# Memory attention's results transposed as f16 halves by DMA instead of by TensorE, and the key-and-value stage's last pair reordered

## The chip, the cores and the metric

The kernel runs on one core of one Trainium2 chip. The metric is the time of one execution on the device in microseconds (us), as the median of several runs. A profile is one execution recorded by the hardware profiler; its times differ slightly from those of the other runs.

## The reference

Two attention layers are computed side by side, and their results are laid beside each other along the last axis. Sequence 2048, width 1024, 32 heads of 32 columns.

```python
# A: memory attention, 4 segments of 512 rows, with M and z carried from segment to segment
for s in range(N):
    qs, ks, vs = q[:, :, s], k[:, :, s], v[:, :, s]
    p = softmax(qs @ ks.T * scale + mask)
    a_dot = p @ vs
    a_mem = (phi(qs) @ M) / (phi(qs) @ z + 1e-6)      # phi(t) = t + 1 if t > 0 else exp(t)
    outs.append(g * a_mem + (1.0 - g) * a_dot)
    M = M + phi(ks).T @ vs
    z = z + phi(ks).sum(rows)
a = stack(outs) @ A_wo
# B: linear attention with learned features, per head
pq, pk = q @ w_phi, k @ w_phi
phi_q = concat(softmax(pq), softmax(-pq)); phi_k = concat(softmax(pk), softmax(-pk))
kv = phi_k.T @ v; z = phi_k.sum(rows)
b = (phi_q @ kv) / (phi_q @ z + 1e-6) @ B_wo
out = concat(a, b)
```

The mask hides the columns behind the diagonal. All matrix products of full width are made from f16 halves: a value is split into a high f16 half and the f16 rest, and a product is the sum of high by high, high by low and low by high, so that three matmuls stand for one.

## The kernel before

**Stages.** (1) Memory attention, in 32 units (`units`): a unit is one segment `s` and one group `g` of four heads. `produce(u)` projects keys, queries and values of a unit, `attend(u)` does its attention and memory. Between them TensorE folds B's feature weights into its key and query weights (`fold`), and prepares forms of weights and inputs. (2) The key-and-value stage of B goes through eight pairs of row blocks in the order `SEQ`; each pair has a key product and a value product by `strassen` (seven products of twelve matmuls for one of 1024x1024x256), `expo` (the two softmaxes) and sums of keys times values (L1435). (3) The query stage goes through the same eight pairs, two chunks `c` each: `strassen` for queries, `expo`, the denominators, a split of the scaled features into f16 halves in the buffer `eh` (L1607, L1610), a DMA that transposes them (L1613, `pt`), a product with the key-value sums (L1622, tiles `pv` and `kv`), and the output product of B (`project`). (4) The final stage makes A's output product in eight row blocks, seven products of twelve matmuls each (L1681, `mult`).

**Order.** A program written in Python plans the order beforehand: each operation has a priority, a planned duration and its dependences, and `Graph.run` chooses for each engine a fixed order by a model of times. The table `MOVES` shifts the priorities of numbered jobs per engine. On the chip every engine goes through its own list in order and waits where a semaphore demands it. All DMAs are issued from SyncE (SP), also in a fixed order, so that a DMA whose input is not ready holds up those behind it.

**What the change touches.** At the end of `attend`, the unit's result `osum` (128 rows by four blocks of 128, f32) is turned by four TensorE transposes into a PSUM bank (L1051), copied by ACT into `oT` (L674) and stored into the scratch tensor `oa_d`. The final stage loads `oa_d` as f32 tiles A0 and A1 (L1646). The buffer tag `oT` has one buffer, which the folding of weights uses as well; the tag `oall` has two. The restacking DMAs (`S<-h`, L840) bring a unit's keys and queries into the layout that its maxima (L882) and scores (L983) read. In stage 2, `VFIRST` names the pair of `SEQ` whose values come ahead of its keys: the last one. `VS` and `KS` are the slots that hold the forms of the value and the key weights; the query weights are loaded into the slots of the one that is free first. `XS` and `XB` are the slots for a pair's input forms.

Of the kernel before, what the change touches and what calls it, by code (L numbers as in the profile page):

```python
# [32 lines left out]
VFIRST = (7,)  # L33
# [23 lines left out]
MOVES = {  # L57
    "DVE": {
# [18 lines left out]
    "ACT": {  # L77
# [6 lines left out]
    "POOL": {  # L84
        42: 1, 95: -4, 100: -5, 147: 2, 148: -1.5, 150: -5, 161: 0.5, 173: 12, 188: 7, 222: -21.5, 240: 2.6, 245: 0.5,
        250: -1.5, 255: -2.5, 257: -2.5, 264: -5.5, 270: -5, 282: -22.5, 326: -8, 328: 2, 341: -2.5, 376: 10.5, 389: -36.5},
# [205 lines left out]
def tile_kernel(ctx: ExitStack, tc: tile.TileContext, ax, aw, awv, awo, beta, bx, bwqk, bwv, bphi, bwo, out):  # L292
# [7 lines left out]
    oa_d = dram.tile([NT, 128, NG, 128], F32, name="oa_d")  # L300
# [29 lines left out]
    nc.vector.memset(one, 1.0)  # L330
    pst = const.tile([128, NT // 2, 5], F32, name="pst")
# [337 lines left out]
    osc = G.fixed(oa_d)  # L669
    wgss, wvss, xscs, wab, wvab, wgbs, wvbs, xams = (G.fixed(t) for t in (wgs, wvs, xsc, wa_d, wva_d, wgb, wvb, xam))  # L670
# [130 lines left out]
    def values(u):  # L801
# [6 lines left out]
        sc = d["sc"] = G.buf("a", [128, 4], F32, "sc", 4)  # L808
        op(POOL, 0.39, lambda: nc.gpsimd.tensor_scalar(sc(), gate1[:, 4 * g:4 * g + 4], bvv()[:, 1, i2:i2 + 1], None, op0=OP.mult),
           r=[gates, (bv, i2)], w=[sc], prio=P + VPRIO)  # L810
        ps = bank("proj", [128, 4, 128])
# [41 lines left out]
    def attend(u):  # L853
# [75 lines left out]
        if s > 0:  # L929
            amem = G.buf("a", [128, 4, 4, 32], F32, "amem", 1)  # L930
            for b in range(2):
# [9 lines left out]
                dve(0.17, lambda dm=dm: nc.vector.reciprocal(dm(), dm()), r=[dm], w=[dm])  # L941
                dve(0.34, lambda ps=ps, dm=dm, b=b: nc.vector.tensor_tensor(
# [102 lines left out]
        if s > 0:  # L1045
            pool(1.15, lambda: nc.gpsimd.tensor_tensor(
                osum(), osum(), amem().rearrange("p c h d -> p c (h d)"), op=OP.add), r=[amem, osum], w=[osum])
        oT = G.buf("a", [128, 4, 128], F32, "oT", 1)
        po = bank("misc", [128, 4, 128], "output")
        for i in range(4):  # L1050
            pe(0.112, lambda i=i: nc.tensor.transpose(po()[:, i, :], osum()[:, i, :], ident), r=[osum], w=[po], need=[oT])  # L1051
# [701 lines left out]
```

## Time and profile before

| what | us |
|---|---|
| runs shown: median (lowest, highest) of 3 | 1688.12 (1687.51, 1689.02) |
| profiled execution: time | 1690.85 |
| profiled execution: span from first to last instruction | 1689.1 |
| memory attention (about 30 to 943 us) | 913 |
| key-and-value stage (about 943 to 1210 us) | 267 |
| query stage (about 1210 to 1545 us) | 335 |
| final stage (about 1545 to 1689 us) | 144 |

The profile names engines PE (TensorE), PEld (its weight loads), DVE (Vector), ACT (Scalar), POOL (GpSimd) and SP (SyncE). A row of a group of instructions reads: line, engine, operation, output and inputs, count, then busy us and mean ns of one, then the idle time of the engine before them and what ended it. "L" numbers are lines of the kernel before.

### The profile page before, as it was taken

The numbers are of one execution on the slowest core, as the hardware profiler recorded it, in microseconds if no ns is written. First come the engines' busy times: TensorE is split into PE (matmuls) and PEld (weight loads), VectorE is DVE, ScalarE is ACT, GpSimd is POOL, SyncE is SP. The second block draws the span as 40 slices with busy tenths as digits, with TensorE's granted clock in tenths as the row PEclk, the third lists the DMA queues.
The fourth block names the chain that finished last, engine by engine and source line by source line (L and its number), as shares of the span: only waits on it lengthen the run. The fifth ranks groups of instructions, "written<-read, shape, count | busy, mean of one in ns | idle before, by whom it ended". The sixth has DMA issues, their size and how long they took to land. (4 is left out here: it accounts for less than half of the span.)

```text
span 1689.1 us, 40231 instructions
## 1 busy us (share of the span) xinstructions
PE 1658.1 (98%) x15176; PEld 995.5 (59%) x15176; DVE 1344.2 (80%) x3198; ACT 1157.4 (69%) x2128; POOL 966.5 (57%) x1285
## 2 busy tenths in 40 slices
PE   8999999999999999999999999999979999999999
PEld 6767667666767767767764454454534444444444
DVE  6889898888998878878974787877978896976441
ACT  7898989878878988777873486765545564454331
POOL 4346578546468885756661576754588888450000
PEclk9999999999999999999999999999989999999999
DMA  7556646655766484864367465467546775865311
GB/s 224 170 170 165 211 141 195 210 174 160 243 195 191 140 223 126 224 188 127 93 179 265 150 219 168 139 205 282 207 97 166 173 202 136 220 140 169 124 57 62
DMA packets 261970, 292.64 MB, mean 173 GB/s; under 512 B 138880, under 2 KB 192896, under 8 KB 255120
## 3 DMA queue, kind: packets, MB, share of 16 engines
q1 hardware_dynamic: 261776, 290.07, 57.5%
q8 instruction: 119, 1.95, 0.5%
q14 instruction: 75, 0.61, 0.1%
HBM read 161.17 MB, written 86.05 MB: 146 GB/s over the span
## 5 line engine op out<-in xcount | busy, mean ns | idle before, releaser
L404 PE MATMUL proj<-S,S 128*128 128x512 f16 (+1 forms) x3072 | 504.3, 300 | 2.8 <-ACT S L437 1.1
L404 PEld LDWEIGHTS <-S 128*128 128x128 f16 x4608 | 333.8, 98 | 154.0 <-issue 7.4
L618 PE MATMUL proj<-S,S 128*128 128x512 f16 x1584 | 362.7, 379 | 0.6 <-ACT cs L624 0.6
L618 PEld LDWEIGHTS <-S 128*128 128x128 f16 x2016 | 192.8, 98 | 220.4 <-issue 1.8
L996 POOL TENSOR_SCALAR_AFFINE_SELECT ph<-ph 128x256 f16<-128x256 f16 (+1 forms) x448 | 192.1, 451 | 139.1 <-DVE ph L990 113.4
L888 DVE CUSTOM_DVE_ANT_0 s<-s,causal 128x256 f32<-128x256 f32 (+3 forms) x512 | 242.7, 509 | 16.7 <-PE s L882 13.3
L990 DVE SCALAR_TENSOR_TENSOR ph<-s,ph 128x512 f16<-128x512 f32 x320 | 209.7, 682 | 40.5 <-ACT ph L989 38.7
L989 ACT ACTIVATE ph<-s 128x512 f16<-128x512 f32 x320 | 189.1, 649 | 0.7
L404 PE MATMUL misc<-S,ot 128*128 128x512 f16 x768 | 175.2, 385 | 0.7 <-ACT ot L1631 0.7
L1281 ACT ACTIVATE e<-e,sk 128x256 f32<-128x256 f32 x256 | 112.3, 496 | 61.5 <-DVE e L1278 59.7
L404 PEld LDWEIGHTS <-ot 128*128 128x128 f16 x768 | 74.4, 99 | 90.7 <-issue 3.4
L983 PE MATMUL s<-S 104*128 104x512 f16 (+3 forms) x512 | 115.7, 299 | 1.9 <-ACT S L910 1.2
L882 PE MATMUL s<-S 96*128 96x512 f16 (+3 forms) x512 | 112.9, 299 | 2.3 <-DVE mt L888 1.4
L987 ACT ACTIVATE s<-s,os 128x512 f32<-128x512 f32 x160 | 105.5, 700 | 13.7 <-PE s L983 13.6
L987 ACT ACTIVATE s<-s,bd 128x512 f32<-128x512 f32 x160 | 106.2, 705 | 7.9 <-PE s L983 6.5
L404 PE MATMUL proj<-wv,S 128*128 128x128 f16 x1536 | 108.4, 219 | 0.0
L1019 PEld LDWEIGHTS <-ph 128*128 128x128 f16 x2560 | 87.1, 96 | 18.0 <-issue 1.9
L1587 POOL TENSOR_TENSOR e<-e,zb 128x512 f32<-128x512 f32 x64 | 84.7, 1341 | 21.8 <-DVE r L1284 18.2
L1019 PE MATMUL pv<-vl,ph 128*128 128x66 f16 (+1 forms) x2560 | 91.9, 184 | 1.0 <-DVE mt L888 0.6
L1284 DVE TENSOR_REDUCE r<-e 128x32 f32<-128x1024 f32 x64 | 76.7, 1205 | 16.3 <-ACT e L1281 16.3
L888 DVE DVE_READ_ACCUMULATOR2_ANT mt<- 128x1 f32 x512 | 72.0, 141 | 0.0
L1393 POOL TENSOR_TENSOR e<-e,r 128x1024 f32<-128x1024 f32 x32 | 61.3, 1920 | 15.4 <-DVE r L1287 11.9
(336 smaller groups left out, 3257.1 us busy)
## 6 DMA issues: line engine op xcount, KB each, us to landing
S<-xf_d SPq DMA_DIRECT2D x126, 256.0 KB
S<-h SPq DMA_DIRECT2D x192, 128.0 KB
S<-wf_d SPq DMA_DIRECT2D x21, 1024.0 KB
st<-bwqk SPq DMA_DIRECT2D x64, 256.0 KB
out<-os SPq DMA_DIRECT2D x40, 256.0 KB
S<-aw SPq DMA_DIRECT2D x16, 512.0 KB
wa_d<-S SPq DMA_DIRECT2D x16, 512.0 KB
wf_d<-fo SPq DMA_DIRECT2D x32, 256.0 KB
```

Source lines behind the costliest of these rows:

```text
L404: op(PE, dur, lambda c=c, a=a, b=b, lv=lv, rv=rv: nc.tensor.matmul(pv(), lv(), rv(), start=(c == 0 and a + b == 0), stop=(c == n - 1 and a ...
L618: op(PE, 0.215, lambda n=n, a=a, b=b, lv=lv, rv=rv: nc.tensor.matmul(ps(), lv(), rv(), start=(start and n == 0 and a + b == 0), stop=(n == ...
L882: nc.tensor.matmul(ps()[:, o:o + 128 * i + 128], st()[0:96, 0, h, 128 * i:128 * i + 128], st()[0:96, 1, h, 0:128 * i + 128], start=True, s ...
L888: dve(0.12 + 0.00113 * n, lambda h=h, i=i, o=o, n=n: nc.vector.tensor_tensor_reduce(ps()[:, o:o + n], ps()[:, o:o + n], causal[:, 512 - n: ...
L983: nc.tensor.matmul(ps()[:, o:o + n], st()[0:104, 1, h, 128 * j:128 * j + 128], st()[0:104, 0, h, 128 * j:512], start=True, stop=True)
L987: act(0.59, lambda: nc.scalar.activation(ps(), ps(), AF.Exp, bias=0.0, scale=bdv()[:, 3, i2, 0:1]), r=[(bd, i2)], w=[ps])
L989: act(0.5, lambda: nc.scalar.activation(ph()[:, 0], ps(), AF.Copy, scale=2.0 ** 14), r=[ps], w=[(ph, 0)])
L990: dve(0.6, lambda: nc.vector.scalar_tensor_tensor(ph()[:, 1], ps(), 2.0 ** 14, ph()[:, 0], op0=OP.mult, op1=OP.subtract), r=[ps, (ph, 0)], ...
L996: nc.gpsimd.affine_select(pd, pd, pattern=[[0, n], [1, 128]], compare_op=OP.is_ge, fill=0.0, base=0, channel_multiplier=-1)
L1019: nc.tensor.matmul(ps()[:, i, n0:n1], ph()[:, a, o:o + 128], vl()[:, j, h, n0:n1], start=(i == 0 and a == 0), stop=(j == min(i, 2)), skip_ ...
L1281: op(ACT, 0.41, lambda i=i: nc.scalar.activation(e()[:, 4 * i:4 * i + 4], e()[:, 4 * i:4 * i + 4], AF.Exp, bias=0.0, scale=sk()[:, i:i + 1 ...
L1587: op(POOL, 1.35, lambda a=a, h0=h0, e=e: nc.gpsimd.tensor_tensor(e()[:, 8 * a:8 * a + 8], e()[:, 8 * a:8 * a + 8], zv()[:, h0:h0 + 8], op= ...
```

## The change

1. In `attend`, ACT and GpSimd split `osum` into f16 halves (`ohl`, under the tag `oall`); one DMA from SP transposes the eight blocks into `oT`, which is now f16, and a second stores it. The four TensorE transposes, their PSUM bank and the copy go. `oa_d` holds halves.
2. So that halves suffice, a unit's result is scaled by `ofs`, the smallest inverse bound of the values over the segments so far: a new Vector operation per unit, a GpSimd multiplication on `sc` in every unit and on `dm` (twice) in units with memory.
3. In the final stage, each of the tiles A0 and A1 is loaded as four pieces of halves into buffers of tag `cs` (two DMAs each for a row half), GpSimd adds the halves, and ACT scales each block of 128 columns by the inverse of `ofs`.
4. `VFIRST` becomes empty: the last pair's keys come ahead of its values. The query weights go to the slots `KS`, and `QSEQ` makes the query stage begin with pair 5, whose input forms lie in place already; the second pair's go to `XQ`. The output weights of B, `eh` and some forms move to other slots. Four subtractions into `eh` go from GpSimd to Vector, and the key-value sums are multiplied by a mask of blocks (`bm2`).
5. `MOVES` is another table, with fewer entries.

```diff
-VFIRST = (7,)
+VFIRST = ()
+XQ = (("S11", 4), ("S15", 3))
+QSEQ = (5, 1, 2, 3, 4, 0, 6, 7)
 MOVES = {
...
-        7: -1829, 11: 1.5, 21: -3.5, 88: 6.5, 94: -7, 97: -3.5, 125: -1, 129: -3, 172: 6, 188: 17.5, 238: -27.5, 250: 8},
+        188: -5, 253: -9.5, 262: -5.5, 388: -12.5},
...
-    oa_d = dram.tile([NT, 128, NG, 128], F32, name="oa_d")
+    oa_d = dram.tile([NSEG, NG, 128, 2, 4, 128], F16, name="oa_d")
...
+            op(DVE, 0.1, lambda: nc.vector.tensor_tensor(ofs[:, s, g:g + 1], ofs[:, s - 1, g:g + 1], bvv()[:, 2, i2:i2 + 1], op=OP.min),
+               r=[(bv, i2), (ofb, (s - 1, g))], w=[(ofb, (s, g))], prio=P + VPRIO)
...
+        op(POOL, 0.39, lambda: nc.gpsimd.tensor_scalar(sc(), sc(), ofs[:, s, g:g + 1], None, op0=OP.mult),
+           r=[(ofb, (s, g))], w=[sc], prio=P + VPRIO)
...
+                pool(0.2, lambda dm=dm: nc.gpsimd.tensor_scalar(dm(), dm(), ofs[:, s, g:g + 1], None, op0=OP.mult), r=[(ofb, (s, g))], w=[dm])
...
-        oT = G.buf("a", [128, 4, 128], F32, "oT", 1)
-        po = bank("misc", [128, 4, 128], "output")
-        for i in range(4):
-            pe(0.112, lambda i=i: nc.tensor.transpose(po()[:, i, :], osum()[:, i, :], ident), r=[osum], w=[po], need=[oT])
-        act(0.48, copy(oT, po), r=[po], w=[oT])
-        op(SP, 0.6, lambda: nc.sync.dma_start(oa_d[4 * s:4 * s + 4, :, g, :].rearrange("c p t -> p c t"), oT()),
+        ohl = G.buf("a", [128, 2, 512], F16, "oall", 2)
+        oT = G.buf("a", [128, 8, 128], F16, "oT", 1)
+        act(0.53, lambda: nc.scalar.activation(ohl()[:, 0], osum().rearrange("p c n -> p (c n)"), AF.Copy), r=[osum], w=[(ohl, 0)])
+        pool(1.28, lambda: nc.gpsimd.tensor_tensor(
+            ohl()[:, 1], osum().rearrange("p c n -> p (c n)"), ohl()[:, 0], op=OP.subtract), r=[osum, (ohl, 0)], w=[(ohl, 1)])
+        op(SP, 1.6, lambda: nc.sync.dma_start_transpose(oT(), ohl().rearrange("p a n -> p (a n)")), r=[ohl], w=[oT], prio=P, lat=1.2, kb=64)
+        op(SP, 0.6, lambda: nc.sync.dma_start(oa_d[s, g].rearrange("p a c t -> p (a c) t"), oT()),
            r=[oT], w=[(osc, u)], prio=P, lat=1.5)
...
-            wqf = load_forms(0, VS, P + 0.1, [])
+            wqf = load_forms(0, KS, P + 0.1, [])
...
-    x, x1 = xkept(0, XS, PB + 12.9), xkept(1, XB, P + 2, True)
+    x1 = xkept(QSEQ[1], XQ, P + 2, True)
...
-                sub, ns, d = (POOL, nc.gpsimd, 1.28) if q and c < 2 else (DVE, nc.vector, 0.7)
-                op(sub, d, lambda q=q, e=e, hv=hv, ns=ns: ns.tensor_tensor(
+                op(DVE, 0.7, lambda q=q, e=e, hv=hv: nc.vector.tensor_tensor(
...
-            op(SP, 0.6, lambda t=t, k=k: nc.sync.dma_start(t().rearrange("p h g t -> p (h g) t"), oa_d[k]),
-               r=[osc], w=[t], prio=P, lat=1.0, kb=512)
+            sg, cc = divmod(k, 4)
+            for h in range(2):
+                raw = G.buf("b", [128, 2, 512], F16, "cs", 4)
+                for a in range(2):
+                    op(SP, 0.6, lambda raw=raw, sg=sg, cc=cc, h=h, a=a: nc.sync.dma_start(
+                        raw()[:, a].rearrange("p (g t) -> p g t", g=4),
+                        oa_d[sg, 4 * h:4 * h + 4, :, a, cc, :].rearrange("g p t -> p g t")),
+                       r=[osc], w=[(raw, a)], prio=P, lat=1.0, kb=128)
+                op(POOL, 1.28, lambda t=t, raw=raw, h=h: nc.gpsimd.tensor_tensor(
+                    t()[:, h].rearrange("p g t -> p (g t)"), raw()[:, 0], raw()[:, 1], op=OP.add), r=[raw], w=[(t, (h, g)) for g in range(4)], prio=P)
+                for g in range(4):
+                    op(ACT, 0.25, lambda t=t, h=h, g=g, sg=sg: nc.scalar.activation(
+                        t()[:, h, g], t()[:, h, g], AF.Copy, scale=ofs[:, sg, 4 * h + g:4 * h + g + 1]), r=[ofb], w=[(t, (h, g))], prio=P)
```

TensorE, at the last unit's result (line L1051 the transposes, L618 matmuls of a value product), before:

```order
L618 LDWEIGHTS S_15383
L618 MATMUL proj<-S_13173,S_15383 128x512
L1051 MATMUL misc<-ident,osum 128x128 x4
L618 LDWEIGHTS S_15383
L618 MATMUL proj<-S_13173,S_15383 128x512
```

Now, behind the last unit's last product of probabilities and values (L1024), with L612 the same value product:

```order
L1024 LDWEIGHTS ph
L1024 MATMUL pv<-vl_120,ph 128x33
L1024 LDWEIGHTS ph
L1024 MATMUL pv<-vl_120,ph 128x66
L612 LDWEIGHTS S_13993
L612 MATMUL proj<-S_12760,S_13993 128x512
```

The transposes are gone, in this unit as in the other 31, and nothing stands in their place on TensorE.

SP, in memory attention, around the store of the eighth unit's result, before (`S_187<-h` the restacking of the next unit's keys and queries, `st` and `S<-ax` loads of weights and inputs):

```order
L840 DMA S_187<-h_4886 32x4x512 x3
L1053 DMA oa_d<-oT 128x4x128
L457 DMA S_4991<-awv 128x2048
L1094 DMA st<-bwqk 128x512 x2
L840 DMA S_187<-h_4886 32x4x512 x2
L1078 DMA wf_d<-fo 1024x1x128
L840 DMA S_187<-h_4886 32x4x512
```

Now, in the same place:

```order
L1058 DMA_TRANSPOSE oT<-oall 128x8x128
L844 DMA S_190<-h_5186 32x4x512 x2
L1059 DMA oa_d<-oT 128x1024
L844 DMA S_190<-h_5186 32x4x512 x3
L1100 DMA st<-bwqk 128x512
L844 DMA S_190<-h_5186 32x4x512
L451 DMA S_5347<-ax 128x2048
```

The transposing DMA stands ahead of the restacking, and the store, which needs the transposed tile, in the midst of it.

SP, at the start of the query stage (`S<-xf_d` input forms of later pairs, `S<-bo_d` output weights of B, `pt` the first transposed tiles), before:

```order
L606 DMA S_15069<-xf_d 128x1024
L1507 DMA S_19558<-bo_d 128x4096
L1507 DMA S_19606<-bo_d 128x4096
L606 DMA S_13808<-xf_d 128x1024
L1613 DMA_TRANSPOSE pt<-S_19649 128x16x128
L606 DMA S_13808<-xf_d 128x1024
L606 DMA S_15069<-xf_d 128x1024
L1613 DMA_TRANSPOSE pt<-S_19649 128x16x128 x3
```

Now:

```order
L1517 DMA S_19575<-bo_d 128x4096
L1517 DMA S_19685<-bo_d 128x4096
L1622 DMA_TRANSPOSE pt<-S_19693 128x16x128 x2
L600 DMA S_13993<-xf_d 128x1024 x2
L600 DMA S_15245<-xf_d 128x1024
L1622 DMA_TRANSPOSE pt<-S_19693 128x16x128 x2
```

The first two transposes stand together now, and three loads stand between them and the third and fourth; before, two loads stood between the first and the second.

More of the change, by code (lines that the diff above doesn't have):

```diff
@@ L57 @@
 MOVES = {
-    "DVE": {
[18 rows of a table removed]
-    "ACT": {
[6 rows of a table removed]
-    "POOL": {
-        42: 1, 95: -4, 100: -5, 147: 2, 148: -1.5, 150: -5, 161: 0.5, 173: 12, 188: 7, 222: -21.5, 240: 2.6, 245: 0.5,
-        250: -1.5, 255: -2.5, 257: -2.5, 264: -5.5, 270: -5, 282: -22.5, 326: -8, 328: 2, 341: -2.5, 376: 10.5, 389: -36.5},
[5 rows of a table added]
+    "DVE": {
[4 rows of a table added]
+    "ACT": {
[3 rows of a table added]
+    "POOL": {
+        28: -3, 62: 0.1, 148: -2.5, 173: -1, 183: -4, 188: -3, 192: -1.5, 203: 1.5, 216: -4.5, 221: 0.5, 238: -1, 254: -2,
+        257: 2, 264: -0.2, 280: 0.5, 325: -1.5, 364: 2.5, 386: -27.5, 388: -131},
+    "SP": {
+        188: -5, 253: -9.5, 262: -5.5, 388: -12.5},
 }
@@ L330, in tile_kernel @@
     nc.vector.memset(one, 1.0)
+    bm2 = const.tile([128, 2], F32, name="bm2")
+    nc.vector.tensor_reduce(bm2, bm.rearrange("p (two h) -> p two h", two=2), axis=AX.X, op=OP.add)
     pst = const.tile([128, NT // 2, 5], F32, name="pst")
@@ L669, in tile_kernel @@
     osc = G.fixed(oa_d)
+    ofs = const.tile([128, NSEG, NG], F32, name="ofs")
+    ofb = G.fixed(ofs)
     wgss, wvss, xscs, wab, wvab, wgbs, wvbs, xams = (G.fixed(t) for t in (wgs, wvs, xsc, wa_d, wva_d, wgb, wvb, xam))
@@ L808, in values @@
         sc = d["sc"] = G.buf("a", [128, 4], F32, "sc", 4)
+        if s == 0:
+            op(DVE, 0.1, lambda: nc.vector.tensor_copy(ofs[:, s, g:g + 1], bvv()[:, 2, i2:i2 + 1]),
+               r=[(bv, i2)], w=[(ofb, (s, g))], prio=P + VPRIO)
+        else:
+            op(DVE, 0.1, lambda: nc.vector.tensor_tensor(ofs[:, s, g:g + 1], ofs[:, s - 1, g:g + 1], bvv()[:, 2, i2:i2 + 1], op=OP.min),
+               r=[(bv, i2), (ofb, (s - 1, g))], w=[(ofb, (s, g))], prio=P + VPRIO)
         op(POOL, 0.39, lambda: nc.gpsimd.tensor_scalar(sc(), gate1[:, 4 * g:4 * g + 4], bvv()[:, 1, i2:i2 + 1], None, op0=OP.mult),
            r=[gates, (bv, i2)], w=[sc], prio=P + VPRIO)
+        op(POOL, 0.39, lambda: nc.gpsimd.tensor_scalar(sc(), sc(), ofs[:, s, g:g + 1], None, op0=OP.mult),
+           r=[(ofb, (s, g))], w=[sc], prio=P + VPRIO)
         ps = bank("proj", [128, 4, 128])
@@ L1501, in project @@
                 out[row:row + 128, col + 512 * n:col + 512 * n + 512], os()), r=[os], prio=prio, lat=1.5)
-    x, x1 = xkept(0, XS, PB + 12.9), xkept(1, XB, P + 2, True)
-    bo = [[G.buf("slot", [128, 2, 4, 512], F16, f"S{4 + 2 * n + q}") for q in range(2)] for n in range(2)]
+    x1 = xkept(QSEQ[1], XQ, P + 2, True)
+    bo = [[G.buf("slot", [128, 2, 4, 512], F16, f"S{2 * n + q}") for q in range(2)] for n in range(2)]
     for n in range(2):
@@ L1555, in tile_kernel @@
         if c % 2 == 0:
-            sk, er = times(c // 2, 0, P - 1.2), {}
+            sk, er = times(QSEQ[c // 2], 0, P - 1.2), {}
             def qout(i, hb, ps, er=er, sk=sk, P=P):
@@ L1562, in tile_kernel @@
             if c + 2 < NT:
-                x = x1 if c == 0 else xkept(c // 2 + 1, XS, P)
+                x = x1 if c == 0 else xkept(QSEQ[c // 2 + 1], XS, P)
         ot = G.buf("b", [128, 2112], F16, "ot", 4)
         if c == 2:
-            for f, i in (("B11", 8), ("T1", 12)):
+            for f, i in (("B11", 11), ("T1", 15)):
                 wform[f] = G.buf("slot", [128, 2, 4, 512], F16, f"S{i}")
```

18 lines of the change are left out of this document (12 added, 6 removed), and 34 rows, old and new, of the table MOVES.

## The prediction

> **What bounds the kernel now.** I read the page first, then the time table by stage, then TensorE's list of waits.
>
> ```profile
> PE 1658.1 (98%) x15176; PEld 995.5 (59%) x15176; DVE 1344.2 (80%) x3198; ACT 1157.4 (69%) x2128; POOL 966.5 (57%) x1285
> 30.00:943.00 913.00, 904.20 (x9565) 629.00 (x9564) 775.84 (x2211) 738.98 (x1326) 556.76 (x858) 1.00 0.61 181
> 943.00:1210.00 267.00, 265.77 (x1915) 136.48 (x1913) 216.68 (x396) 180.53 (x374) 169.28 (x161) 1.00 0.58 196
> 1545.00:1689.10 144.10, 140.07 (x649) 63.29 (x647) 55.28 (x81) 46.94 (x71) 0.00 (x0) 1.00 0.24 86
> PE s L882 <- DVE mt L888: 1.4, 2, 0.9
> PE pv L1622 <- DMA pt<-S: 11.3, 3, 7.4
> ```
>
> The first row is the page's; the next three are the table (stretch, length, busy time of PE, PEld, DVE, ACT, POOL, granted clock, share of the DMA engines, GB/s); the last two are the longest wait of TensorE inside 30 to 943 us and the longest of all. TensorE (PE) is busy 904.2 of 913 us in the memory-attention stage and 265.8 of 267 in the key stage, at full clock. The kernel is a queue of TensorE work: what takes work off TensorE shortens it, what an idle engine does costs nothing, and the one place where TensorE stands still is the start of the query stage, where it waits for transposing DMAs. Vector (DVE) is next, with 137 us to spare in the attention stage.
>
> **The change part by part.** The sum is made against the profiled execution, 1690.85 us (span 1689.1 and 1.75 around it); the median of the runs shown, 1688.12, lies 2.73 lower, and I carry the difference over to it.
>
> *Transposes off TensorE.* Rows of TensorE around one unit's four transposes (start, length, kind):
>
> ```profile
> 151.63 0.60 PE L404 MATMUL proj<-S,S 128*128 128x512 f16 x2
> 152.06 0.60 PE L1051 MATMUL misc<-ident,osum 128*128 128x128 f32 x4
> 152.50 1.00 PE L404 MATMUL proj<-S,S 128*128 128x128 f16 x15
> ```
>
> The printed length overlaps the next matmul; from start to next start the four hold TensorE 152.50 - 152.06 = 0.44 us. All 32 units lose them: 32 x 0.44 = **14.1 us** on the path, if what is queued behind is ready. The order of TensorE has no other matmul more or less.
>
> [...]
>
> *What takes their place.* The pieces of work that the nearest rows price:
>
> ```profile
> L1046 POOL TENSOR_TENSOR osum<-osum,amem 128x512 f32<-128x512 f32 x24 | 31.9, 1327 | 12.3 <-DVE osum L1042 11.2 <-DVE amem L942 1.1
> L1040 POOL TENSOR_TENSOR rd<-rd,sc 128x16 f32<-128x16 f32 x32 | 8.1, 252 | 23.2 <-DVE rd L1039 18.3 <-DVE mh L903 3.9 <-DVE wvs L419 0.9
> L674 ACT ACTIVATE oT<-misc 128x512 f32<-128x512 f32 x32 | 20.0, 624 | 5.2 <-PE misc L1051 4.8 <-issue 0.2
> L939 DVE TENSOR_SCALAR dm<-misc 128x8 f32<-128x8 f32 x48 | 6.8, 155 | 7.6 <-PE misc L935 7.2
> L1281 ACT ACTIVATE e<-e,sk 128x256 f32<-128x256 f32 x256 | 112.3, 496 | 61.5 <-DVE e L1278 59.7 <-DVE d L1595 1.4 <-DVE e L1276 0.2
> ```
>
> GpSimd (POOL) gets, over the stage, 32 subtractions at 1.33 and 80 small multiplications at 0.25: 62.6 us into 356 idle. Scalar (ACT) swaps a copy of 0.62 for another of the same form. Vector gets 32 small operations at 0.16: 5 us into 137. All of that is hidden by TensorE's work. The new multiplication of dm stands between two Vector operations on a PSUM bank and can hold Vector for a GpSimd turn; Vector's spare covers it, and uncovered it would cost at most 48 x 0.25 = 12 us.
>
> On SyncE's queue (SP) each unit gets a DMA that transposes eight 128x128 blocks, and its store must wait until that has landed; the restacking DMAs of the next unit's keys and queries (S<-h) stand behind the pair. The trace shows transposing DMAs of sixteen blocks:
>
> ```profile
> L1613 SPq DMA_TRANSPOSE pt<-S x32: 1594/2263/5292, 1227.0 to 1520.2; - x32
> 1239.94 10.83 SPq L1613 DMA_TRANSPOSE pt<-S  x3
> 1244.54 0.26 PE L1622 MATMUL pv<-pt,kls 64*32 64x128 f16 x1 [7.40 <-DMA pt<-S]
> 1242.00:1244.00 2.00, 0.00 (x0) 0.00 (x0) 0.45 (x1) 0.00 (x0) 2.00 (x4) 0.50 1.14 209
> ```
>
> From issue to the matmul that waited for it are 1244.54 - 1239.94 = 4.6 us, with the DMA engines full at 209 GB/s. Half the blocks hold SP between 2.3 (in proportion) and 4.6 us (all of it latency); I take 3.5. Counted in the order at this trace's 0.216 us for 512 columns, the new kernel leaves TensorE work of at least 7.9 us (median 15.9) between the end of a unit's query projection and its first maxima; before it is 7.7 and 16.5. A hold of 3.5 us fits even the tightest place if the restack takes no more than 4. The stage's idle time on TensorE is 913 - 904.2 = 8.8 us; I let it grow by 1 (0 to 8.8: at the worst it doubles).
>
> *The start of the query stage.* What it costs now:
>
> ```profile
> 1234.71 0.23 PE L1622 MATMUL pv<-pt,kls 64*32 64x128 f16 x1
> 1235.24 1.90 PE L618 MATMUL proj<-S,S 128*128 128x512 f16 x8
> 1247.61 0.26 PE L1622 MATMUL pv<-pt,kls 64*32 64x128 f16 x1 [2.22 <-DMA pt<-S]
> 1248.38 4.45 PE L404 MATMUL misc<-S,ot 128*128 128x512 f16 x10
> 1238.00:1240.00 2.00, 0.00 (x0) 0.00 (x0) 2.00 (x5) 0.64 (x2) 1.33 (x1) 0.89 0.00 0
> 1250.00:1252.00 2.00, 2.00 (x6) 0.76 (x5) 0.49 (x3) 2.00 (x6) 1.84 (x3) 0.50 1.04 198
> 1252.00:1254.00 2.00, 2.00 (x7) 0.75 (x6) 1.43 (x2) 0.75 (x2) 2.00 (x3) 0.69 1.21 72
> ```
>
> Two waits, 7.40 and 2.22 us; then the granted clock is 0.50 until some 1252.7. Ten matmuls take 4.45 us where eight took 1.90 (ten: 2.3), so half clock costs 2.1, and some 0.6 on two groups of small matmuls. Together **12.3 us**.
>
> With keys ahead of values, the last pair's key sums are done while TensorE still has value and query work: between them and the first transposed group stand 162 matmuls of 512 columns instead of 117, 9.7 us more. But what the wait ends on is Vector, which was hardly idle before it. In before, from the sum that completes the first query product to the end of the first subtraction ahead of the transpose:
>
> ```profile
> 1189.88 0.68 DVE L628 TENSOR_TENSOR proj<-cs,proj 128x512 f32<-128x512 f32 x1
> 1225.27 0.68 DVE L1610 TENSOR_TENSOR S<-e,S 128x512 f16<-128x512 f32 x1
> 1189.90:1225.90 36.00, 34.15 (x65) 1.00 0.57 205
> ```
>
> That is 36.1 us, 34.2 of it busy. In the new order the same stretch of Vector holds four more sums of denominators, two more additions of partial products, two subtractions of kls, one more of S (GpSimd did it) and one more maximum, and lacks two subtractions of pt and some short ones: by starts of rows of these kinds, 0.60 us apart, 4.1 us more. So the first transpose can be issued after 40.2 us and land after 44.8. TensorE reaches the first transposed group after 168 matmuls x 0.216, 60 small ones of the sums and 16 of zb: about 39.9. It waits about 5 us there, and at a wait of that length the clock falls again (it had fallen within 2.6 us of idleness): 3 us more. The second group's transpose follows directly on SP instead of behind two loads, so it is hidden. Left over 8 of 12.3: **4.3 us** gained; bounds 12.3 (Vector keeps up, no wait) and 0.
>
> *Final stage.* Each of eight row blocks now adds halves: 32 additions of GpSimd at 1.33 (42.6 us into 144 idle) and 128 scalings on ACT of 128 columns, at most 0.496 (twice the columns) and at least 0.25, half of that: 32 to 64 us into 97. Steady state stays TensorE's. Only the first blocks are at risk, whose chain is longer by one addition and four scalings, 2.6 us, in a busy spell: 1.4 us, bounds 0 and 5.
>
> Sum: -14.1 - 4.3 + 1 + 1.4 = -16.0: 1674.9 for a profiled execution, **1672** as a median.
>
> **The rivals.** *Clean start of the query stage:* Vector's idle 2 us and stretched operations in that window don't recur, the wait is gone: -14.1 - 12.3 + 2.4, 1664. For: keys come 84 matmuls earlier. Against: the count above.
>
> *A worse start:* the third and fourth groups stand together behind one loading DMA that must see TensorE finish; a second wait of 7 us: 1679.
>
> *The work goes and the time does not:* Vector or the SP hold set the pace of the attention stage and the 14.1 us become idle time; the start's gain alone remains: 1684 to 1688. Against it: Vector has 15% to spare there.
>
> *Slower:* the SP hold comes as the longest issue in the row, 5.29 us, plus 4.6 of landing, 9.9 us a unit. With 5 us for the restack (an estimate from the copy, the subtraction and a DMA) a unit needs 15; half of the 32 have less, by some 3.5 us on average: 56 us lost, and if half of the restacks escape by standing ahead of the transpose, 28. Result 1700 to 1728. It decides from 0.5 us lost per unit (16 / 32). For it: SP serves everything in order. Against it: in the query stage as many transposes, twice as large, in a third of the time, made TensorE wait three times.
>
> [...]
>
> **How the numbers follow.** My forecast 0.55, clean start 0.17, worse start 0.08, no gain in attention 0.08, slower 0.12. A measurement of this kernel can tell about 0.2% (3.4 us) from no change. Faster: the first three and a quarter of the fourth, 0.82; same 0.06; slower 0.12. The likeliest is 1672. The range goes from 1661 (clean start with nothing given back) to 1686 (most of the fourth case); outside it lie the slower case and little else.
>
> **What would show it.** Right: TensorE's row of L1051 gone and its busy time about 1644; the stage of attention ending near 930 instead of 943; one wait of about 5 us for pt at the first transposed group, with the clock at 0.50 behind it; GpSimd busy about 43 us in the last 140. Wrong: waits of "PE s" for the DMA S<-h or for Vector's mt of 10 us and more in sum, an SP queue that stands at the store of oT many times over 5 us, or no wait at all for pt.

## The result, and the profile after

The changed kernel takes 1698.88 us (median of 4 runs, 1698.62 to 1699.58), the kernel before 1688.57 beside it (1687.51 to 1689.07): a ratio of 1.0061, 95% interval 1.0048 to 1.0074. It is slower by 10.3 us, where 16 us less had been forecast. Lines of the new kernel differ a little: maxima on Vector L892 (before L888), scores L988 (L983), weight products L398 (L404), first product of the query stage L1631 (L1622), products of the final stage L1703 (L1681).

The page's row of engines and the table by stage of the kernel after, with the columns as before; the third and fourth stretch begin at the first product of the query stage and of the final stage.

```profile
PE 1650.1 (97%) x15048; PEld 984.2 (58%) x15048; DVE 1383.7 (82%) x3238; ACT 1190.2 (70%) x2256; POOL 1071.2 (63%) x1425
30.00:943.00 913.00, 886.83 (x9372) 613.75 (x9370) 782.51 (x2227) 732.13 (x1318) 619.12 (x967) 0.99 0.66 186
943.00:1246.00 303.00, 300.41 (x2073) 151.97 (x2071) 254.63 (x458) 192.70 (x402) 187.50 (x185) 1.00 0.58 191
1246.00:1532.00 286.00, 280.30 (x2739) 129.75 (x2737) 247.42 (x392) 159.03 (x321) 222.03 (x227) 1.00 0.70 174
1532.00:1697.00 165.00, 157.43 (x720) 70.67 (x720) 78.39 (x103) 83.84 (x181) 30.55 (x24) 0.99 0.32 91
```

All 128 transposes are gone, and yet TensorE stands idle for 26.2 of 913 us in the attention stage, where it was 8.8. Up to the first product of the query stage the table reads, first before, then after:

```profile
0.00:1234.70 1234.70, 1219.69 (x11724) 794.16 (x11724) 1036.83 (x2706) 954.33 (x1762) 752.44 (x1063) 1.00 0.60 185
0.00:1246.85 1246.85, 1212.91 (x11592) 783.91 (x11593) 1058.75 (x2746) 947.63 (x1756) 819.51 (x1177) 0.99 0.64 188
```

TensorE is idle 33.9 us there instead of 15.0, 18.9 more. It is busy 6.8 us less and not 14.1, because some of what is left runs at half clock: in stretches of 10 us between 30 and 940 us the granted clock is below 1.00 in four of after (0.83 at 230, 0.66 at 460, 0.80 at 820, 0.86 at 830) and in none of before, an estimated (0.17 + 0.34 + 0.20 + 0.14) x 10 = 8.5 us lost. So the mark comes 18.9 - 6.8 = 12.1 us later. Some of these stretches, first after, then before:

```profile
200.00:210.00 10.00, 8.58 (x102) 6.39 (x100) 9.96 (x20) 9.32 (x18) 5.62 (x8) 1.00 0.41 110
230.00:240.00 10.00, 7.14 (x73) 6.00 (x72) 6.88 (x20) 9.40 (x18) 7.81 (x13) 0.83 0.82 233
300.00:310.00 10.00, 7.77 (x75) 4.97 (x75) 9.94 (x32) 10.00 (x18) 7.61 (x16) 1.00 0.62 159
450.00:460.00 10.00, 7.01 (x51) 4.08 (x50) 9.93 (x32) 6.80 (x12) 4.67 (x7) 1.00 0.60 185
460.00:470.00 10.00, 9.18 (x98) 7.35 (x97) 8.48 (x23) 7.44 (x14) 5.66 (x12) 0.66 0.71 195
820.00:830.00 10.00, 5.98 (x48) 5.23 (x46) 9.93 (x22) 3.98 (x7) 7.98 (x9) 0.80 0.36 119
830.00:840.00 10.00, 10.00 (x116) 8.25 (x114) 8.44 (x31) 1.69 (x3) 2.97 (x5) 0.86 0.25 66
```

```profile
450.00:460.00 10.00, 10.00 (x139) 8.94 (x137) 9.97 (x30) 9.39 (x17) 6.82 (x11) 1.00 0.41 94
820.00:830.00 10.00, 10.00 (x155) 8.90 (x155) 9.15 (x25) 10.00 (x20) 6.31 (x14) 1.00 0.11 35
```

TensorE is idle for more than 1 us in ten such stretches. In six of them Vector (third busy column) is full, 9.9 or more (200, 300, 350, 370, 450, 820); in three it has 8.8 to 9.3, and at 230 it has 6.9 and waits itself, 1.96 us, for ACT. Vector was as full before at 450, but TensorE had its operands there. So the 137 us that Vector has to spare in the stage are an average; mostly they do not lie where they are needed. By TensorE's list of waits, Vector ends some 22 of 25 us of its longer waits in this stage. The longest of the whole span and one of the shorter rows:

```profile
PE misc L1130 <- DVE mt L892: 4.0, 1, 4.0
PE s L988 <- DVE mt L892: 3.4, 5, 1.4
PE proj L1703 <- DVE ot L433: 2.9, 1, 2.9
PE s L988 <- DVE ph L995: 2.4, 2, 2.3
PE pv L1631 <- DMA pt<-S: 1.9, 3, 1.2
PE s L886 <- DVE mt L892: 1.6, 1, 1.6
```

No row of the list names the restacking DMAs. The start of the query stage is clean (1.9 us for pt in the whole query stage, where it was 11.3), but comes at 1246.85 instead of 1234.71. The largest single wait has a cause of its own, in the time table of after (start, length, engine):

```profile
820.96 1.27 POOL L1195 TENSOR_TENSOR S<-S 128x512 f32<-128x512 f32 x1
821.25 4.46 DVE L906 TENSOR_SCALAR mh<-mt 128x16 f16<-128x16 f32 x1
822.19 1.16 POOL L1206 TENSOR_TENSOR fp<-S,fp 128x512 f16<-128x512 f32 x1
823.30 1.27 POOL L1195 TENSOR_TENSOR S<-S 128x512 f32<-128x512 f32 x1
824.52 1.16 POOL L1206 TENSOR_TENSOR fq<-S,fq 128x512 f16<-128x512 f32 x1
826.69 2.08 PE L1130 MATMUL misc<-phib,st 128*128 128x128 f32 x8 [4.02 <-DVE mt L892]
```

A Vector operation on 16 columns, whose 31 other instances take 0.16 to 0.99 us, lasts 4.46 and ends when a run of four GpSimd operations ends (824.52 + 1.16 = 825.68). What held it for that long is not shown by any run.

### The profile page after: what moved, and what is told of

It reads as the page before. It is cut to its first block, busy times and chain, and to the rows that moved or that the text cites. A ratio compares the mean times of both kernels' runs of the same rounds, so it can differ in the third digit from the quotient of the medians.

```text
span 1697.0 us, 40343 instructions
## 1 busy us (share of the span) xinstructions
PE 1650.1 (97%) x15048; PEld 984.2 (58%) x15048; DVE 1383.7 (82%) x3238; ACT 1190.2 (70%) x2256; POOL 1071.2 (63%) x1425
## 3 DMA queue, kind: packets, MB, share of 16 engines
q8 instruction: 118, 1.93, 0.5%
## 4 chain that ended last, share of the span: by engine, by line
PE 68%; DVE 17%; ACT 7%; DMA 3%; issue 3%; POOL 2%; DVEq 0%; SPq 0%; ACTq 0%; POOLq 0%
PE proj L398 17%; PE proj L612 17%; PE misc L398 8%; PE proj L1703 5%; DVE s L892 3%; PE s L612 3%; PE s L988 3%; PE s L1703 2%; PE pv L1024 2%; PE s L886 2%; DVE ph L995 2%; ACT s L992 2%; ACT ph L994 2%; PE misc L612 2%; DVE S L433 1%
## 5 line engine op out<-in xcount | busy, mean ns | idle before, releaser
L398 PE MATMUL proj<-S,S 128*128 128x128 f16 (+1 forms) x3072 | 504.6, 300 | 7.2 <-ACT S L431 1.9
L398 PEld LDWEIGHTS <-S 128*128 128x128 f16 x4608 | 332.4, 99 | 157.0 <-issue 15.2
L612 PE MATMUL proj<-S,S 128*128 128x512 f16 x1584 | 366.6, 379 | 1.6 <-ACT cs L618 1.0
L612 PEld LDWEIGHTS <-S 128*128 128x128 f16 x2016 | 191.8, 98 | 218.7 <-issue 3.2
L1001 POOL TENSOR_SCALAR_AFFINE_SELECT ph<-ph 128x256 f16<-128x256 f16 (+1 forms) x448 | 196.0, 459 | 134.1 <-DVE ph L995 119.7
L892 DVE CUSTOM_DVE_ANT_0 s<-s,causal 128x512 f32<-128x512 f32 (+3 forms) x512 | 242.7, 507 | 13.1 <-PE s L886 9.3
L398 PE MATMUL misc<-S,ot 128*128 128x512 f16 x768 | 170.8, 379 | 2.5 <-DVE ot L1642 1.7
L398 PEld LDWEIGHTS <-ot 128*128 128x128 f16 x768 | 73.7, 98 | 91.2 <-DVE ot L1642 3.2
L988 PE MATMUL s<-S 104*128 104x512 f16 (+3 forms) x512 | 117.2, 302 | 6.4 <-DVE mt L892 3.4
L398 PE MATMUL proj<-wv,S 128*128 128x128 f16 x1536 | 105.9, 222 | 0.1
L1024 PEld LDWEIGHTS <-ph 128*128 128x128 f16 x2560 | 88.1, 96 | 20.7 <-issue 3.7
L1024 PE MATMUL pv<-vl,ph 128*128 128x66 f16 (+1 forms) x2560 | 92.4, 185 | 2.8 <-DVE ph L995 1.3
L1619 DVE TENSOR_TENSOR S<-e,S 128x512 f16<-128x512 f32 x64 | 71.9, 1165 | 8.7 <-ACT S L1617 8.7
L1665 POOL TENSOR_TENSOR e<-cs 128x512 f32<-128x512 f16 x32 | 42.2, 1336 | 57.7 <-DVE h L433 24.4
```

Of the source, the lines that this page charges most:

```text
L398: op(PE, dur, lambda c=c, a=a, b=b, lv=lv, rv=rv: nc.tensor.matmul(pv(), lv(), rv(), start=(c == 0 and a + b == 0), stop=(c == n - 1 and a ...
L612: op(PE, 0.215, lambda n=n, a=a, b=b, lv=lv, rv=rv: nc.tensor.matmul(ps(), lv(), rv(), start=(start and n == 0 and a + b == 0), stop=(n == ...
L892: dve(0.12 + 0.00113 * n, lambda h=h, i=i, o=o, n=n: nc.vector.tensor_tensor_reduce(ps()[:, o:o + n], ps()[:, o:o + n], causal[:, 512 - n: ...
L988: nc.tensor.matmul(ps()[:, o:o + n], st()[0:104, 1, h, 128 * j:128 * j + 128], st()[0:104, 0, h, 128 * j:512], start=True, stop=True)
L1001: nc.gpsimd.affine_select(pd, pd, pattern=[[0, n], [1, 128]], compare_op=OP.is_ge, fill=0.0, base=0, channel_multiplier=-1)
L1024: nc.tensor.matmul(ps()[:, i, n0:n1], ph()[:, a, o:o + 128], vl()[:, j, h, n0:n1], start=(i == 0 and a == 0), stop=(j == min(i, 2)), skip_ ...
```

## The experiments

A kernel "in its own order" is planned with every operation; what it leaves out is only not issued, so that all else stands in the order it had. Medians are set beside the runs of the kernel before on the same chip (1688.6 to 1689.9). One profiled execution of most kernels can lie 2 or 3 us from its median.

**The transposes alone.** First, before without them:

```diff
-pe(0.112, lambda i=i: nc.tensor.transpose(po()[:, i, :], osum()[:, i, :], ident), ...)
-act(0.48, copy(oT, po), ...)
+pe(0.112, lambda: None, ...)
+act(0.48, copy(oT, osum), ...)
```

> The kernel before, in its own order, with the 128 TensorE transposes of the results left out and nothing put in their place: ACT copies osum itself, so the output of A stays unturned. It prices the first term of the sum alone. If TensorE is the only bound of the attention stage, the time falls by 14.1 us, to about 1674.5. Rival, the pace of Vector: TensorE's freed time turns into waits for Vector (mt, ph), and no more than half of it comes through: 1681 to 1686.

1686.75 us; ratio 0.9983 [0.9973, 0.9993]. Of 14.1 us some 2 come through. The trace shows one way in which they go (its execution, 1689.90 us, is the second slowest of the twelve runs, so the median lost less than this one). TensorE's time table, and ACT's row ahead of the wait, first before, then without transposes:

```profile
151.40 0.39 PE L983 MATMUL s<-S 104*128 104x384 f16 x2
153.33 0.67 PE L935 MATMUL misc<-mem,pq 128*128 128x132 f32 x4
187.95 0.39 PE L908 MATMUL misc<-identr,mh 128*8 128x128 f16 x4
187.19 1.91 ACT L479 ACTIVATE wv<-S 128x2048 f16<-128x2048 f32 x1 [0.84 <-DMA S<-awv]
875.21 0.39 PE L908 MATMUL misc<-identr,mh 128*8 128x128 f16 x4 [0.37 <-DVE mh L903]
```

```profile
149.74 0.39 PE L983 MATMUL s<-S 104*128 104x384 f16 x2
151.42 0.72 PE L935 MATMUL misc<-mem,pq 128*128 128x132 f32 x4
185.86 0.39 PE L908 MATMUL misc<-identr,mh 128*8 128x128 f16 x4
187.65 1.91 ACT L479 ACTIVATE wv<-S 128x2048 f16<-128x2048 f32 x1 [2.95 <-DMA S<-awv]
190.83 0.42 PE L983 MATMUL s<-S 104*128 104x512 f16 x1 [2.19 <-ACT S L910]
192.00:193.00 1.00, 1.00 (x11) 0.97 (x10) 0.41 (x4) 1.00 (x2) 0.00 (x0) 0.50 1.10 176
875.74 0.39 PE L908 MATMUL misc<-identr,mh 128*8 128x128 f16 x4 [0.34 <-DVE mh L903]
```

At one unit the same two rows lie 1.93 us apart before and 1.68 without the transposes: 0.25 of 0.44 is gained there. At 188 TensorE is 2.09 us ahead. Then it waits 2.19 us for the rows of maxima. Vector and TensorE have done their part of these earlier than before; ACT, which copies them (L910), is not ready, since in its list L479 stands ahead, and the weights that L479 reads are no sooner there than before: ACT waits 2.95 us for their DMA instead of 0.84. Behind the wait TensorE runs at half clock (the stretch's clock column is 0.50). At the next unit it is 1.80 us behind (221.45 instead of 219.65), and at 875 still 0.53. The work went; the time did not. In the other direction, each transpose issued twice:

```diff
-... nc.tensor.transpose(po()[:, i, :], osum()[:, i, :], ident) ...
+... [nc.tensor.transpose(po()[:, i, :], osum()[:, i, :], ident) for _ in range(2)] ...
```

> The kernel before, its order kept, with each of the 128 transposes issued twice. If TensorE alone sets the attention stage, 14.1 us more: 1702.9. Rival: taking the transposes away gave 2 us of 14, since TensorE and Vector wait for each other in turn; if that holds upward too, Vector's chain hides part: 1692 to 1698. If the order had just been fitted to TensorE's load with no room on that side, adding costs the full 14 although removing gains nothing.

1699.18 us, 10.5 more: less than the 14.1 of one theory and more than the other allowed. TensorE's work counts upward, 0.33 us a unit; downward the others are next at once.

**Vector relieved.** In 384 of 512 maxima 128 columns are left out, which only changes softmax's shift; for other inputs that shift could be too small, so it is a probe and no version to keep.

```diff
-ps()[:, o:o + n], ps()[:, o:o + n], causal[:, 512 - n:512], 1.0, NEG, OP.add, OP.max,
+ps()[:, o + n - m:o + n], ps()[:, o + n - m:o + n], causal[:, 512 - m:512], 1.0, NEG, OP.add, OP.max,   # m = max(128, n - 128)
```

> The kernel before, its order kept, with 384 of Vector's 512 maxima (L888) reading 128 columns fewer (the block farthest from the diagonal is left out of the maximum): at 0.14 us for 128 columns some 54 us less of Vector in the attention stage, nothing else changed. It is the base for the next two. If TensorE alone sets the stage it gains no more than the 8.8 us that TensorE stands idle there: 1680 to 1688.

> The same with the 128 transposes left out too. Theory: the transposes' time went into waits for Vector, which the fixed order makes TensorE meet a moment earlier; with Vector relieved the transposes are worth 10 to 14 us against the run before this one (they were worth 2). Rival: ACT, a DMA or the order itself sets the pace; then they are worth 2 to 4 here too.

> The kernel after, its order kept, with the same shorter maxima. Theory Vector: after's 17 us of added idle time and 8 us of half clock are waits for Vector, and most of them go: 20 us or more under after, 1672 to 1679, and below before with the same maxima. Rival: GpSimd's added work and the order hold it up whatever Vector has to do; then it gains no more than before does, 1688 to 1695.

Before: 1685.42 us (0.9976 [0.9966, 0.9985]). Without transposes too: 1675.91 (0.9930 [0.9916, 0.9945]): with Vector relieved the transposes are worth 9.5 us instead of 2. After: 1683.24 (0.9962 [0.9948, 0.9976]), 15.6 less than without the probe and 2.2 under before with it; that lies between what the two theories named. So in after Vector's work costs time, in before hardly any (3.6 us). That the 9.5 us had been lost to waits for Vector alone is not shown: the longest of these waits was ACT's, behind a load. Vector got 39 us less in sum (the row of before with the probe, beside 1344.2), where I had estimated 54:

```profile
PE 1655.4 (98%) x15176; PEld 994.2 (59%) x15176; DVE 1304.9 (77%) x3198; ACT 1157.2 (69%) x2128; POOL 969.2 (58%) x1285
```

**What was added in attention, in after's order.** `stripped` does not issue GpSimd's subtractions and multiplications and stores twice instead of transposing; `no_dma_transpose` leaves out the transposing DMA alone; `after_fused` keeps everything but has one operation do the work of two.

```diff
 # after_fused
-nc.gpsimd.tensor_scalar(sc(), gate1[...], bvv()[:, 1, i2:i2 + 1], None, op0=OP.mult)
-nc.gpsimd.tensor_scalar(sc(), sc(), ofs[...], None, op0=OP.mult)
+nc.gpsimd.tensor_scalar(sc(), gate1[...], bvv()[:, 1, i2:i2 + 1], ofs[...], op0=OP.mult, op1=OP.mult)
-nc.gpsimd.tensor_scalar(dm(), dm(), ofs[...], None, op0=OP.mult)
-nc.vector.tensor_tensor(amem()[...], ps()[...], dm()[...], op=OP.mult)
+nc.vector.scalar_tensor_tensor(amem()[...], ps()[...], ofs[...], dm()[...], op0=OP.mult, op1=OP.mult)
```

> The kernel after, its order of every engine kept, with what the change added to the attention stage left out: GpSimd's 32 subtractions and 80 small multiplications are not issued, and instead of transposing, SP stores the high half twice as it is (so A's part of the output is neither scaled nor turned). [...] Rival, pace and order: the waits on Vector's mt and ph stay where the order puts them, and only the one held operation (4.0 us of wait and its spell at half clock) goes: 1692 to 1698.

> The kernel after, its order kept, with the 32 transposing DMAs alone left out: SP stores the two halves unturned, GpSimd works as in after. By my prediction's hold of SP (3.5 us a unit) or its slower rival (9.9), 5 to 25 us come back: 1674 to 1694. Rival: no wait of TensorE in after's list names a restacking DMA, so nothing comes back: 1697 to 1700.

> The kernel after, its order kept, with GpSimd's 80 small multiplications by ofs folded into operations that run anyway (sc: one GpSimd operation with two factors; dm: the Vector product that follows takes ofs as its scalar). GpSimd loses 26 us of work and Vector no longer waits for a GpSimd turn between the reciprocal and the product. Theory small steps: leaving out all of GpSimd's added work gave 8.4 us, and these turns are most of it: 1691 to 1694. Rival: the 32 subtractions (38 us) make it: 1697 to 1699.

`stripped` 1690.51 us (1.0008 [1.0000, 1.0017]), `no_dma_transpose` 1698.35 (1.0054 [1.0041, 1.0067]), `after_fused` 1694.18 (1.0032 [1.0022, 1.0041]). The transposing DMA costs nothing that can be measured, although SP stands for it in after (the list of SP's waits, and the line's own row with its issue times in ns, least, median, longest):

```profile
SPq L1059 <- DMA oT<-oall: 25.3, 17, 5.7
L1058 SPq DMA_TRANSPOSE oT<-oall x32: 1242/1282/5863, 90.1 to 930.1; - x32
```

The shortest way from its issue to the issue of the store behind it, which waits until it has landed, is 3.1 us (174.97 to 178.06, with nothing between on SP). Without all that GpSimd got (and the transposing DMA) 8.4 us come back, without the 80 small operations 4.7. Part of this shows in Vector's waits: in after it waits for the multiplications of dm (sum, times, longest), in `stripped` and `after_fused` it does not.

```profile
DVE amem L947 <- POOL dm L946: 3.5, 7, 0.8
```

In `after_fused` the operation that had stood for 4.46 us came 0.81 us behind the start of a GpSimd operation instead of 0.29, and ended with that one (820.57 + 1.27 = 821.84), in 0.49:

```profile
820.57 1.27 POOL L1196 TENSOR_TENSOR S<-S 128x512 f32<-128x512 f32 x1
821.38 0.49 DVE L907 TENSOR_SCALAR mh<-mt 128x16 f16<-128x16 f32 x1
821.80 1.15 POOL L1207 TENSOR_TENSOR fp<-S,fp 128x512 f16<-128x512 f32 x1
```

So a start half a microsecond later went with 0.49 us instead of 4.46; why it went on through four operations is open. With TensorE's wait and the half clock behind it (0.80 and 0.86 in two stretches of 10 us, 3.4 us) it is an estimated 7.4 us. It is gone in both runs, so it may be most of these 8 us, and I cannot separate it from the rest. Most of the other holes are not GpSimd's. In `stripped`, without its added work and without transposes, TensorE is still idle for 20.1 of the 913 us, and at 50, 200, 230, 300, 350 and 450 us it stands still for more than 1 us as in after; the holes at 310, 370, 700 and 820 are gone:

```profile
30.00:943.00 913.00, 892.87 (x9408) 615.11 (x9406) 781.57 (x2231) 734.42 (x1324) 557.71 (x855) 0.99 0.59 179
```

That is more the rival's case, the order, though the run came out 1.5 us under its range.

**Final stage.** `after_no_scaling` does not issue ACT's 128 scalings in the final stage.

```diff
-lambda ...: nc.scalar.activation(t()[:, h, g], t()[:, h, g], AF.Copy, scale=ofs[...])
+lambda: None
```

> The kernel after, its order kept, without ACT's 128 scalings in the final stage (A's result stays scaled by ofs). TensorE's waits for ot at the first block, 4.3 us in sum with some half clock, follow a chain of load, GpSimd's addition, four scalings, and the forms. If the scalings make that wait: 1694 to 1696. Rival: the loads and additions make it, 1698 to 1699.

1700.05 us (1.0065 [1.0052, 1.0078]): nothing comes back.

**The parts, and the tables.** Each part alone, and after with the other kernel's table for the attention jobs:

```diff
 # start_alone: only these parts of the diff; MOVES of before for jobs under 237, of after from 237
-VFIRST = (7,)
+VFIRST = ()
+QSEQ = (5, 1, 2, 3, 4, 0, 6, 7)   # with its slots, bm2 and the subtractions on Vector
 # attention_alone: the rest of the diff; MOVES the other way round
 # after_old_table: after; MOVES of before for jobs under 237
```

> The kernel before with part 4 of the change alone (last pair's keys first, query stage begins with pair 5, other slots), the attention and final stages as before; table of before up to the end of attention, table of after behind it. After's trace shows 2.5 us of idle TensorE and full clock around the first transposed groups, where before had 9.6 us and a spell at half clock. If the parts add up, this alone gains 12 to 13 us: 1676. Rival: the start is clean in after only because its attention stage ends otherwise; then the gain is what I forecast, 4 us, 1684.

> The kernel before with parts 1 to 3 of the change alone (transposing DMA, halves, additions in the final stage), with the table of after up to the end of attention and that of before behind it; start of the query stage as before. If the parts add up, it has after's loss without after's gain: 1698.9 + 12.5 = 1711. Rival: attention loses only together with part 4, then 1690 or less.

> The kernel after with the table MOVES of before for the jobs of the attention stage (the numbers name the same jobs in both). Theory order: the attention stage loses its 14 us and more through the sparser new table; with the old one most of the 17 us of added idle time and the 8 us of half clock are gone, 1675 to 1685. Rival operations: what was added (GpSimd work, SP's transposing DMA) makes the waits, under either table: 1695 to 1705.

1692.45 us (1.0019 [1.0010, 1.0029]), 1721.95 (1.0185 [1.0168, 1.0202]) and 1742.47 (1.0314 [1.0296, 1.0333]). All three missed both theories: parts that cost 4 and 33 us alone cost 10 together. A table's shifts were fitted to one plan; beside another plan such a run may price the misfit and not the part. So the same without any table:

```diff
-MOVES = {...}
+MOVES = {}
```

> The kernel after with an empty table MOVES; the kernel before with an empty table runs beside it. With before's table in its attention stage after took 1742. If the change as such is good and only the table is missing a like fit, after without a table beats before without one by 10 us or more; if the added operations cost what the transposes gave, it is equal or slower. Both should be slower than with their tables, 1720 to 1760.

> The kernel before with an empty table MOVES, to set beside after with an empty table (1716.9). If the change as such is good and the table hides it, this one is 10 us or more slower than that: 1727 or more. If the added operations cost what was taken away, it is equal or faster, 1705 to 1717.

> The kernel before with part 4 of the change alone and an empty table; before with an empty table took 1722.1. If the new start is a gain by itself, 1710 or less (12 us); if it is one only through the table, 1718 to 1726.

> The kernel before with parts 1 to 3 of the change alone and an empty table; before with an empty table took 1722.1, after 1716.9. If the parts add up with a start worth 12 us, this one is 7 us slower than before: 1729. If parts 1 to 3 give what I forecast (13 us less 1.4), 1710.

And before's table for the attention jobs alone, with the old start and with the new one:

```diff
 # before_early_table, start_alone_early_table: MOVES of before for jobs under 237, none behind
```

> The kernel before with its table for the jobs of the attention stage alone, and none behind it. From the first product of the query stage to the end, before without any table took 446.1 us and with it 450.4; up to that product 1271.4 and 1234.7. If the table's 33 us are earned in the attention stage, this one takes 1681 to 1690; if the key stage and what lies behind it earn a part, 1695 to 1710.

> The same with part 4 of the change (the new start of the query stage). If the new start is a gain by itself, it lies 7 us under the run before this one, as without a table, 1676 to 1684, and under both kernels; if it was one only in an unfitted order, they are equal.

| kernel | median us | first query product | first final product | last TensorE end |
|---|---|---|---|---|
| before | 1688.57 | 1234.7 | 1529.5 | 1685.1 |
| after | 1698.88 | 1246.8 | 1532.6 | 1692.9 |
| before, no table | 1722.05 | 1271.4 | 1572.3 | 1717.5 |
| new start alone, no table | 1715.09 | 1260.4 | 1563.6 | 1708.8 |
| attention alone, no table | 1719.98 | 1260.2 | 1566.2 | 1716.6 |
| after, no table | 1716.91 | 1253.8 | 1562.4 | 1707.6 |
| before, table for attention alone | 1690.15 | 1237.2 | 1539.2 | 1684.4 |
| new start, before's table for attention alone | 1684.25 | 1232.6 | 1534.5 | 1679.7 |

(The marks are from each profile, one execution: that of before lies 2.3 us above its median, that of after without a table 3.4 below.) Without tables the change is a gain of 5.1 us; the start alone gains 7.0 and the rest alone 2.1, which do not add up, but each is known only to some 3 us. All four runs without a table fell between the values that their expectations named. Up to the first query product the attention part gains 11.2 there (1271.4 to 1260.2), not far from the 13 forecast for that stage; behind it 10.3 are lost (446.1 to 456.4). Before's table is worth 33.5 us (1722.05 - 1688.57), the new one 18.0 (1716.91 - 1698.88); the difference, 15.4, turns -5.1 into +10.3. (The table of before has 260 entries, 178 of them for the attention jobs, that of after 144 and 84.) Before's entries for the attention jobs alone give 1690.15, as good as the whole table (1.0005 [0.9997, 1.0014]): that is where it earns its 33 us. The new start beside this table takes 1684.25, and beside after's late entries it took 1692.45: 8.2 us by late entries alone. The marks agree: up to the first query product before's table buys 36.7 us and the new one 7.0. The last kernel, 1684.25, is faster than both: 0.9969 [0.9959, 0.9980] of before, 14.6 us under after. It has the attention stage of before, TensorE idle for 8.2 us of 913 (its table by stage):

```profile
30.00:943.00 913.00, 904.77 (x9563) 628.68 (x9561) 774.91 (x2209) 739.44 (x1328) 556.36 (x858) 1.00 0.61 181
```

## Why the prediction was wrong, point by point

*Transposes off TensorE, 14.1 us.* The step that failed. The price of 0.44 us was that of work on TensorE, and the clause "if what is queued behind is ready" was not fulfilled: in before's own order 2 us came through, with Vector relieved 9.5. The stage's idle time, which I let grow by 1 us (8.8 at the worst), grew by 17.4, and some 8.5 went to half clock, for which the sum has no term in that stage. I had read "TensorE busy 904 of 913" as one bound; the attention stage has several (TensorE, Vector, ACT and the loads that ACT waits for), and freed time of one meets the next within a few units. The case that I gave 0.08 ("the work goes and the time does not") is what happened when the transposes alone were taken out; its argument against, Vector's 15% to spare, is an average over the stage. The changed kernel fared worse than that case: its first query product came 12.1 us later.

*The table.* A second step was missing altogether: the change brings another order of the attention stage, with fewer entries, and the sum has no term for it. I had counted only that TensorE has as much work between a unit's projection and its maxima as before. By the runs without tables the tables' difference, 15.4 us, is the largest term of the result, and with `stripped` they point to the order as most of the loss. Whether a fuller table would fit the changed kernel as well as before's fits before was not tried.

*What takes their place.* SP's hold is harmless, as forecast (+1, measured 0 for the DMA), and with it the "slower" case falls: it had the sign but not the mechanism. My 3.5 us for the eight blocks stands beside 3.1 where nothing lay between, and SP itself is held 1.28 us by the issue in the median, 5.86 at most. GpSimd's work was costed at nothing because it had 356 us idle; leaving it out gives 8 us back. Waits of Vector for dm, 3.5 us in sum, and the stall above are what the trace shows of it; their shares in the 8 are open.

*Start of the query stage.* -4.3 forecast; measured -5.9 with before's attention table (1690.15 to 1684.25) and -7.0 without a table. That the size is near is luck. The wait of 5 us at the first transposed groups that I worked out from Vector's row isn't there, neither in after (0.3 us for pt up to 1300) nor in the kernel that took 1684.25 (none up to 1500): the rival of a clean start had this right. But it did not bring its whole 12.3; that last kernel waits 5.3 us for pt in two waits behind 1500 us, where before, from 1262 us on, waits 1.7. Before without its late entries has no wait of 7.4 us either (TensorE's waits for pt in that kernel, sum, times, longest) and is no faster: it waits 3.1 us for pt at the start, where 31 matmuls from 1241.32 on then take 8.86 us (0.29 each, where 12 ahead of the wait took 2.75, 0.23 each), and 6.1 later:

```profile
PE pv L1598 <- DMA pt<-S: 9.2, 5, 3.3
```

*Final stage.* +1.4 forecast; from its first product to the end after takes 160.3 us, before 155.6: +4.7. The row of its products in after shows 4.3 us of idle time ahead of them, in two waits at the stage's start; the second row is that of GpSimd's additions:

```profile
L1703 PE MATMUL proj<-S,ot 128*128 128x512 f16 x192 | 46.2, 390 | 4.3 <-DVE ot L433 2.9 <-ACT ot L431 1.4
L1665 POOL TENSOR_TENSOR e<-cs 128x512 f32<-128x512 f16 x32 | 42.2, 1336 | 57.7 <-DVE h L433 24.4 <-DVE ot L433 13.2 <-DMA cs<-oa_d 9.6
```

Without the scalings it is as long (161.0), so they are not what makes the waits. That leaves the loads, the additions and Vector beside them, which no run separates. Vector's subtraction of the second half takes 1.64 us while GpSimd adds (four additions from 1531.52 to 1536.91), and took 0.74 before (first before, then after):

```profile
1533.52 0.74 DVE L439 SCALAR_TENSOR_TENSOR h<-e,osc,h 128x512 f16<-128x512 f32 x1
1534.27 1.64 DVE L433 SCALAR_TENSOR_TENSOR h<-e,osc,h 128x512 f16<-128x512 f32 x1
```

By the marks of the kernels without tables the whole change adds nothing here (145.2 us as before), parts 1 to 3 alone 5.2 (150.4).

*Signs that I named.* Right: the row of the transposes gone. GpSimd's additions are the 42.2 us that I had counted, but only 30.6 us of GpSimd lie behind 1532, the rest ahead of it. Wrong: TensorE's busy time (1650 instead of 1644, by the half clock), the end of attention (the first query product comes 12 us later), and the wait of 5 us for pt. Of the signs against me, SP stood at the store of oT 17 times, 25.3 us in sum and 5.7 at most, not many times over 5; waits of "PE s" for mt came to 5.0 us in sum, under the 10 that I had set: many smaller waits on several producers did it, for which I had set no sign.

## What to carry to other kernels

In a kernel whose order was fitted, the busiest engine being at 99% doesn't make its work the price of the time (here 14.1 us of it were worth 2): take the work out in the same order first (plan it, don't issue it) and see what comes through. A table of hand-fitted shifts belongs to one program; with a change it must be priced as a term of its own, by running both kernels without any, and a part is never to be judged beside the other part's table. And look for spare time of the second engine in stretches of 10 us, not over a stage, and follow a wait back through the queue of the engine that ended it: the longest one in the run without transposes led through ACT to a load.

## What was unexpected in the hardware

In after a Vector operation of 16 columns stood 4.46 us through a row of four GpSimd operations, and TensorE's wait of 4.0 us behind it (PE misc for DVE mt) is in `no_dma_transpose` too; in `after_fused`, where the operation came later within the first of the four, it took 0.49. A unit's eight 128x128 blocks of f16 were transposed by DMA with no loss of time that could be measured (1698.88 us with these DMAs, 1698.35 without), though SP was held for each of them, 1.28 us in the median, and the DMA engines were 66% busy in that stage.
